# Regrouping VectorE's operations by operand memory while weights are split, with u in PSUM in steps 8 to 21

## The chip, the cores and the metric

The kernel runs on one core of a Trainium2 chip. The core has a matrix engine (PE; its weight loads are shown as PEld), VectorE (DVE), ScalarE (ACT), GpSimd (POOL) and SyncE (SP), which only starts DMAs here. Each engine runs its own list of instructions in order, and semaphores make one wait for another. SBUF is the on-chip memory; PSUM is the smaller memory that PE writes its products into, in eight banks of 512 fp32 columns. POOL works on SBUF alone in this kernel. The metric is the device time of one execution in microseconds (us).

## What is computed

Retention attention on 8 sequences of 576 positions with 8 heads of 64, then a feed-forward layer with a rational activation on the 4608 tokens:

```python
scores = scale * np.matmul(q, k.transpose(0, 1, 3, 2))
Dmat = np.where(rel >= 0, gamma[:, None, None] ** rel[None, :, :], 0.0)
x = np.matmul(scores * Dmat, v)            # then heads side by side: 4608 x 512
h = x @ w_in                               # 512 x 2048
P = a[0] + a[1] * h + a[2] * h**2 + a[3] * h**3
Q = 1.0 + np.abs(b[0]) * np.abs(h) + np.abs(b[1]) * h**2
out = (P / (Q + 1e-6)) @ w_out             # 2048 x 512
```

## The kernel before

All large products are done in a split form: a matrix is kept as a rounded part (hi) and the remainder (lo), and hi·hi, lo·hi and hi·lo are summed. The weights come as 8-byte words and are converted and split on the chip while the first steps already run.

**Steps.** The feed-forward part is a list of steps (b, f): 512 tokens (block b) by 128 columns of w_in (f). Steps 0 to 7 are block 0 with f 0 to 7, steps 8 to 23 block 1 with f 0 to 15, then block 0's other half, then blocks 2 to 8. Step i issues `gemm1` (12 matmuls into a PSUM bank h, two buffers), the activation, and `gemm2` of the step three or four earlier (12 matmuls into acc). The activation of a step:

- `ffn_p`: ACT p = a3·h + a2 and u = |h|; DVE p = p·h ("p·h")
- `ffn_p2`: DVE p = (p + a1)·h ("p2")
- `ffn_v`: ACT v = |b1|·u + |b0|; DVE v = v·u ("v·u")
- `ffn_r`: ACT Ln of v into u, then Exp of u into u (a first reciprocal of Q)
- `ffn_q`: three DVE operations, p = (p + a0)·u, v = (v + 1)·u, p = (v - 2)·p ("q1, q2, q3")
- `ffn_hi`, `ffn_lo`: ACT copies p, rounded, into g's first half; in steps up to 25 POOL, later DVE, subtracts for the second half. g's pool has three buffers.

**Splitting a weight** (`split_weight`) is a generator whose five pieces are `start` (ACT, Abs of the words' high halves into c), `split0` ("shift": one DVE TENSOR_SCALAR on c), `split1` ("low": bits and c), `split2` ("high": bits and c), and `split3` (ACT copies c, rounded, into w, POOL subtracts for w's second half). One or two weights are begun in each step up to 23 (`STARTS`). All operands lie in SBUF.

**Attention** comes in 36 units of 128 positions. `scores` (PE into PSUM ps), `decay` (DVE, ps times a mask into s), in the next step `outputs` (48 small matmuls in the profile), `keep_hi` (ACT, the rounded part into xhi), `keep_lo` (DVE, xlo, and the state S_sb), `fade` (POOL scales S_sb), `scale_q` (POOL) and `scale_v` (ACT, eight instructions on kv). Units 5, 6 and 7 have their scores in steps 1, 3 and 5 and their outputs in steps 2, 4 and 6; unit 4's outputs are in step 0, and unit 8 follows in steps 23 and 24. The pool `ps_at` holds one such ps of two PSUM banks (some early units use `ps_acc`).

**What sets the order.** The lists at the top (lines 33 to 45) are walked in each step by `run`, and each name issues its instructions on the engines it uses; `InOrder` keeps every engine in that order. FIRST holds for steps 0 to 23, DENSE up to step 31, REST after it. Tiles are taken from pools by tag; u and v have two buffers each, p three. The tile framework adds the waits: from what was written to and read from a tile.

Of the kernel before, what the change touches and what calls it, by code (L numbers as in the profile page):

```python
# [12 lines left out]
F32 = mybir.dt.float32  # L13
# [8 lines left out]
P = 128  # L22
# [9 lines left out]

BEFORE = "scale_q split1 scale_v split2 split3 start scores outputs decay split0 keep_hi keep_lo fade".split()
FIRST = (
    "split1 gemm1 outputs ffn_p split2 ffn_hi keep_hi ffn_lo gemm2 ffn_r scale_q split3 keep_lo fade start ffn_p2"
    " scale_v scores decay split0 ffn_q ffn_v"
).split()
DENSE = (
    "gemm1 outputs keep_hi split1 keep_lo fade ffn_p split2 split0 ffn_v scale_q ffn_hi ffn_r ffn_lo scale_v gemm2"
    " ffn_p2 scores decay split3 ffn_q"  # L40
).split()
REST = (
    "gemm1 ffn_p outputs keep_hi keep_lo fade ffn_hi ffn_p2 ffn_lo scores decay scale_q scale_v ffn_v gemm2 ffn_r ffn_q"
).split()
END = "ffn_r ffn_hi gemm2 ffn_lo ffn_q".split()

# [3 lines left out]
SCORES = [1, 3, 5, 23, 25, 27, 29, *range(2 * NF, (NB - 1) * NF, 4)]  # L50
# [16 lines left out]
def retention_ffn(ctx: ExitStack, tc: tile.TileContext, qkv, w_in, w_out, ab, masks, gq, gv, out):  # L67
# [20 lines left out]
    ps_at = ctx.enter_context(tc.tile_pool(name="ps_at", bufs=1, space=PSUM))  # L88
# [184 lines left out]
    els = {}  # L273
    gs = {}
    accs = {}
    part = []
    spare = {}

# [11 lines left out]
    def ffn_p(b, f):  # L290

        h = hs[b, f]
        u, v, p = els[b, f] = [
            (el3 if t == "p" else el).tile([P, 512], F32, tag=t, name=f"{t}{b}_{f}") for t in "uvp"
        ]
        act.activation(p, h, AF.Identity, bias=a2, scale=a3)
        act.activation(u, h, AF.Abs)
        dve.tensor_tensor(p, p, h, ALU.mult)
# [2 lines left out]
        p = els[b, f][2]  # L301
        dve.scalar_tensor_tensor(p, p, a1, hs.pop((b, f)), ALU.add, ALU.mult)

    def ffn_v(b, f):

        u, v, p = els[b, f]
        act.activation(v, u, AF.Identity, bias=b0, scale=b1)
        dve.tensor_tensor(v, v, u, ALU.mult)

    def ffn_r(b, f):  # L310
# [67 lines left out]
    half = NF // 2  # L378
    first = half + NF
    runs = [(0, 0, half), (1, 0, NF), (0, half, NF)] + [(b, 0, NF) for b in range(2, NB)]  # L380
    steps = [(b, f, f == r0, f == r1 - 1) for b, r0, r1 in runs for f in range(r0, r1)]
    at = {s[:2]: i for i, s in enumerate(steps)}

    def lag(i):

        return 4 if NF // 2 <= i < first - 2 or i >= len(steps) - 8 else 3
# [6 lines left out]
    def load_weights(n):  # L393
        for k in [k for _, k in zip(range(n), loads)]:
            load_weight(k)
# [12 lines left out]
    def run(names, todo):  # L408
        todo |= {f"split{j}": (split_step, j) for j in range(4)}
        for name in names:  # L410
            if name in todo:
                todo[name][0](*todo[name][1:])
# [39 lines left out]
    for i in range(len(steps) + lag(len(steps))):  # L452
        this, prev, prev2 = (steps[j][:2] if 0 <= j < len(steps) else None for j in (i, i - 1, i - 2))
        todo = {"gemm2": (products, i), "start": (split_start, STARTS[i] if i < first else 0)}

        out_n = None
        if due and this:
            out_n = due.pop()
            todo |= {f.__name__: (f, out_n) for f in (keep_hi, keep_lo, fade)}
            todo["outputs"] = (put_out, out_n)  # L460
        if i in SCORES:
            todo |= {f.__name__: (f, nxt) for f in (scores, decay)}
            due.append(nxt)
            nxt += 1
        if i + 1 in SCORES:
            todo |= {f.__name__: (f, nxt) for f in (scale_q, scale_v)}
        if this:
            todo |= {f.__name__: (f, *this) for f in (gemm1, ffn_p, ffn_p2, ffn_v)}
        if prev:
            todo |= {f.__name__: (f, *prev) for f in (ffn_r, ffn_q)}  # L470
        if prev2:
            todo |= {"ffn_hi": (ffn_hi, *prev2), "ffn_lo": (ffn_lo, *prev2, i - 2 < first)}
        run(END if not this else FIRST if i < first else DENSE if i < 2 * NF else REST, todo)
        load_weights(2)

# [40 lines left out]
```

## Time and profile before

| | |
|---|---|
| Median of 3 runs | 1001.1 us (1000.58 to 1001.1) |
| The profiled execution | 999.55 us, of which the span from first to last instruction is 997.8 |
| PE busy | 934.3 us (94%) |
| DVE busy | 839.0 us (84%) |
| ACT busy | 709.0 us (71%) |
| POOL busy | 158.3 us (16%) |
| Mean granted TensorE clock | 0.978 |

The engines overlap, so busy times don't add up to the span. What counts is which engine is never free in a stretch of the program, and what the others wait for there. All kernel instructions carry line 63, that of the helper which records them, so they are told apart by the names of their tiles.

### The profile page before, as it was taken

How to read it: one execution, taken by the hardware profiler on the slowest of the kernel's cores; microseconds unless marked ns; L12 is line 12 of the kernel's file. 1: busy time of each engine (PE TensorE's matmuls, PEld its weight loads, DVE VectorE, ACT ScalarE, POOL GpSimd, SP SyncE). 2: the span in 40 equal slices, each digit the busy share in tenths (PEclk: the TensorE clock that was granted, in tenths of full speed). 3: DMA queues.
4: the chain of work that ended last, by engine and by line, in shares of the span. 5: the costliest groups of instructions: out<-in, count | busy, mean ns of one | idle time of the engine just before them, and what ended most of it. 6: DMA issues, size and time to landing. Idle time of an engine off the chain costs nothing.

```text
span 997.8 us, 14766 instructions
## 1 busy us (share of the span) xinstructions
PE 934.3 (94%) x5658; PEld 756.3 (76%) x5658; DVE 839.0 (84%) x1189; ACT 709.0 (71%) x1274; POOL 158.3 (16%) x128
## 2 busy tenths in 40 slices
PE   5687878788999999999999999999999999999998
PEld 5566766566787888878888888888878888888886
DVE  3499989999788888888888888988888888888895
ACT  4386777777767777777777777777777777777774
POOL 2444433443100000100000000100000000000000
PEclk8798999999999999999999999999999999999999
DMA  9943100002212111210121112111211121001001
GB/s 359 407 178 127 43 0 1 1 0 82 89 43 85 44 43 43 85 64 22 43 85 43 43 44 85 43 43 43 85 43 43 43 85 44 1 1 43 1 1 42
DMA packets 20550, 65.31 MB, mean 65 GB/s; under 512 B 2304, under 2 KB 2432, under 8 KB 20480
## 3 DMA queue, kind: packets, MB, share of 16 engines
q1 hardware_dynamic: 20480, 64.37, 17.9%
q8 instruction: 44, 0.72, 0.3%
q14 instruction: 26, 0.21, 0.1%
HBM read 54.93 MB, written 9.44 MB: 65 GB/s over the span
## 4 chain that ended last, share of the span: by engine, by line
PE 73%; DVE 16%; ACT 5%; issue 3%; DMA 2%; POOL 0%; SPq 0%; ACTq 0%; POOLq 0%
PE acc L63 33%; PE h L63 31%; PE ps L63 9%; DVE c L63 7%; DVE p L63 6%; DVE v L63 2%; DMA qk<-in_qkv 2%; ACT c L63 1%; ACT u L63 1%; ACT kv L63 1%; ACT o L63 1%; ACT v L63 1%; DMA kv<-in_qkv 1%; ACT g L63 0%; POOL qk L63 0%
## 5 line engine op out<-in xcount | busy, mean ns | idle before, releaser
L63 PE MATMUL acc<-w,g 128*128 128x512 f32 x1632 | 404.9, 397 | 5.2 <-ACT o L63 4.0
L63 PE MATMUL h<-xhi,w 128*128 128x512 f32 x1152 | 381.1, 392 | 17.9 <-DVE p L63 17.2
L63 PEld LDWEIGHTS acc<-w,g 128*128 128x128 f32 x1632 | 305.2, 190 | 77.4 <-ACT o L63 4.8
L63 PEld LDWEIGHTS h<-xhi,w 128*128 128x128 f32 x1152 | 216.5, 188 | 69.4 <-DVE p L63 22.7
L63 PE MATMUL h<-xlo,w 128*128 128x512 f32 x576 | 224.6, 390 | 0.2 <-DVE xlo L63 0.2
L63 ACT ACTIVATE p<-h,ab_sb 128x512 f32<-128x512 f32 x144 | 111.4, 773 | 135.2 <-PE h L63 135.1
L63 DVE TENSOR_TENSOR v<-v,u 128x512 f32<-128x512 f32 x144 | 124.4, 864 | 27.9 <-ACT v L63 27.9
L63 DVE SCALAR_TENSOR_TENSOR p<-p,ab_sb,u 128x512 f32<-128x512 f32 x144 | 108.8, 756 | 27.2 <-ACT u L63 26.4
L63 ACT ACTIVATE u<-h 128x512 f32<-128x512 f32 x144 | 85.7, 595 | 61.8 <-DVE v L63 60.4
L63 DVE TENSOR_TENSOR p<-p,h 128x512 f32<-128x512 f32 x144 | 98.9, 687 | 33.9 <-ACT u L63 33.2
L63 PEld LDWEIGHTS h<-xlo,w 128*128 128x128 f32 x576 | 108.3, 188 | 22.4 <-DVE xlo L63 0.5
L63 ACT ACTIVATE v<-u,absb 128x512 f32<-128x512 f32 x144 | 116.2, 807 | 1.3 <-DVE p L63 1.1
L63 POOL TENSOR_TENSOR S_sb<-S_sb,gv_sb 128x256 f32<-128x256 f32 x32 | 21.8, 680 | 583.3 <-DVE S_sb L63 583.3
L63 DVE SCALAR_TENSOR_TENSOR p<-p,ab_sb,h 128x512 f32<-128x512 f32 x144 | 107.2, 744 | 3.1
L63 ACT ACTIVATE u<-u,lnb 128x512 f32<-128x512 f32 x144 | 104.4, 725 | 4.7
L63 DVE SCALAR_TENSOR_TENSOR p<-v,p 128x512 f32<-128x512 f32 x144 | 101.6, 706 | 5.0
L63 ACT ACTIVATE u<-v,lnb 128x512 f32<-128x512 f32 x144 | 103.1, 716 | 0.1
L63 DVE SCALAR_TENSOR_TENSOR v<-v,u 128x512 f32<-128x512 f32 x144 | 99.4, 690 | 0.0
L63 ACT ACTIVATE g<-p 128x512 fp32r<-128x512 f32 x136 | 85.7, 630 | 8.0 <-DVE p L63 4.3
L63 DVE TENSOR_TENSOR g<-p,g 128x512 fp32r<-128x512 f32 x112 | 77.6, 693 | 1.4 <-ACT g L63 1.4
L63 ACT ACTIVATE kv<-kv,gv_sb 128x64 f32<-128x64 f32 x288 | 72.5, 340 | 6.2 <-DMA gv_sb<-in_gv 5.0
L63 POOL TENSOR_TENSOR qk<-qk,gq_sb 128x512 f32<-128x512 f32 x36 | 59.7, 1660 | 9.5 <-DMA qk<-in_qkv 9.5
(35 smaller groups left out, 634.6 us busy)
## 6 DMA issues: line engine op xcount, KB each, us to landing
qk<-in_qkv SPq DMA_DIRECT2D x36, 512.0 KB, 4.8
kv<-in_qkv SPq DMA_DIRECT2D x36, 512.0 KB, 3.9
bits<-in_w_in SPq DMA_DIRECT2D x16, 512.0 KB, 10.2
bits<-in_w_out SPq DMA_DIRECT2D x16, 512.0 KB, 10.2
out<-o SPq DMA_DIRECT2D x16, 512.0 KB, 3.2
out<-o SPq DMA_DIRECT2D x4, 256.0 KB, 2.3
gq_sb<-in_gq SPq DMA_DIRECT2D x1, 256.0 KB, 2.7
mask_sb<-in_masks SPq DMA_DIRECT2D x1, 128.0 KB, 4.5
```

The source lines that it names most:

```text
L63: return lambda *a, **k: self.tc.keep_in_program_order(method(*a, **k))
```

## The change

Three things are changed. The order FIRST is a new one, in which `scores` and `decay` stand last, `outputs` stays near the front, and the three DVE pieces of a split follow each other behind `ffn_q`. In steps up to 23 `ffn_r` works on the step's own u and v, not on those of the step before, and `ffn_hi` on the step before, not on the one before that; step 24 then has neither. And in steps 8 to 21 u is one of the two halves (banks) of a tile free_at, which is taken from `ps_at` in step 8 and given up in step 22. `ffn_v` is cut in two, `ffn_va` (ACT) and `ffn_v` (DVE); in DENSE and REST the two stand together.

```diff
 FIRST = (
-    "split1 gemm1 outputs ffn_p split2 ffn_hi keep_hi ffn_lo gemm2 ffn_r scale_q split3 keep_lo fade start ffn_p2"
-    " scale_v scores decay split0 ffn_q ffn_v"
+    "gemm1 outputs ffn_p ffn_lo keep_hi split3 ffn_va ffn_p2 ffn_v keep_lo fade ffn_r start ffn_q ffn_hi"
+    " split0 split1 split2 scale_q scale_v gemm2 scores decay"
 ).split()
...
+    free_at = []
...
         u, v, p = els[b, f] = [
+            free_at[f % 2] if t == "u" and free_at else
             (el3 if t == "p" else el).tile([P, 512], F32, tag=t, name=f"{t}{b}_{f}") for t in "uvp"
         ]
...
-    def ffn_v(b, f):
+    def ffn_va(b, f):
 
         u, v, p = els[b, f]
         act.activation(v, u, AF.Identity, bias=b0, scale=b1)
+
+    def ffn_v(b, f):
+        u, v, p = els[b, f]
         dve.tensor_tensor(v, v, u, ALU.mult)
...
-            todo |= {f.__name__: (f, *prev) for f in (ffn_r, ffn_q)}
+            todo["ffn_q"] = ffn_q, *prev
+
+        if i != first and (this if i < first else prev):
+            todo["ffn_r"] = ffn_r, *(this if i < first else prev)
+        if i != first and (prev if i < first else prev2):
+            todo["ffn_hi"] = ffn_hi, *(prev if i < first else prev2)
         if prev2:
-            todo |= {"ffn_hi": (ffn_hi, *prev2), "ffn_lo": (ffn_lo, *prev2, i - 2 < first)}
+            todo["ffn_lo"] = ffn_lo, *prev2, i - 2 < first
+        if i == half:
+            ps = ps_at.tile([P, 2, 512], F32, tag="at", name="free_at")
+            free_at.extend((ps[:, 0], ps[:, 1]))
+        elif i == SCORES[3] - 1:
+            free_at.clear()
```

Three places in the built order show it. The first is DVE in step 12 (block 1, f = 4) before: the rows of one step, each with the semaphores that it waits for in brackets (Activation is ACT's).

```order
L63 SCALAR_TENSOR_TENSOR c_11_1199<-bits_11_862,c_11_1199 128x512 [waits DMAHW7_49]
L63 TENSOR_TENSOR p_4_1228<-p_4_1228,h_4_1213 128x512 [waits Activation_49,Pool_49]
L63 SCALAR_TENSOR_TENSOR c_11_1199<-bits_11_862,c_11_1199 128x512 [waits DVE_49]
L63 SCALAR_TENSOR_TENSOR p_4_1228<-p_4_1228,ab_sb,h_4_1213 128x512 [waits DVE_49]
L63 TENSOR_SCALAR c_8_1255<-c_8_1255 128x512 [waits Activation_49]
L63 SCALAR_TENSOR_TENSOR p_3_1170<-p_3_1170,ab_sb,u_3_1168 128x512
L63 SCALAR_TENSOR_TENSOR v_3_1169<-v_3_1169,u_3_1168 128x512
L63 SCALAR_TENSOR_TENSOR p_3_1170<-v_3_1169,p_3_1170 128x512 [waits DVE_49]
L63 TENSOR_TENSOR v_4_1227<-v_4_1227,u_4_1226 128x512 [waits Activation_49]
```

The same step in the changed kernel:

```order
L63 TENSOR_TENSOR p_4_1229<-p_4_1229,h_4_1215 128x512 [waits Activation_49,Pool_49]
L63 SCALAR_TENSOR_TENSOR p_4_1229<-p_4_1229,ab_sb,h_4_1215 128x512 [waits DVE_49]
L63 TENSOR_TENSOR v_4_1228<-v_4_1228,free_at 128x512 [waits Activation_49]
L63 SCALAR_TENSOR_TENSOR p_3_1172<-p_3_1172,ab_sb,free_at 128x512 [waits Activation_49]
L63 SCALAR_TENSOR_TENSOR v_3_1171<-v_3_1171,free_at 128x512
L63 SCALAR_TENSOR_TENSOR p_3_1172<-v_3_1171,p_3_1172 128x512 [waits DVE_49]
L63 TENSOR_SCALAR c_8_1242<-c_8_1242 128x512 [waits Activation_49]
L63 SCALAR_TENSOR_TENSOR c_8_1242<-bits_8_952,c_8_1242 128x512 [waits DMAHW0_49,DVE_49]
L63 SCALAR_TENSOR_TENSOR c_8_1242<-bits_8_952,c_8_1242 128x512 [waits DVE_49]
```

The c rows have moved from between p's rows to the end of the step, and the row that forms p_3 from u (q1), which had no wait, now waits for ACT.

The second place is ACT in the same step of the changed kernel (g_3 and p_3 are the step before's; w_11 is a weight that was begun in the step before).

```order
L63 ACTIVATE p_4_1229<-h_4_1215,ab_sb 128x512 [waits PE_49,Pool_49]
L63 ACTIVATE free_at<-h_4_1215 128x512 [waits Activation_49]
L63 ACTIVATE w_11_1234<-c_11_1185 128x512 [waits DVE_49,Activation_49]
L63 ACTIVATE v_4_1228<-free_at,absb 128x512 [waits Activation_49]
L63 ACTIVATE free_at<-v_4_1228,lnb 128x512 [waits DVE_49]
L63 ACTIVATE free_at<-free_at,lnb 128x512 [waits Activation_49]
L63 ACTIVATE c_8_1242<-bits_8_952 128x512 [waits DMAHW0_49]
L63 ACTIVATE g_3_1247<-p_3_1172 128x512 [waits DVE_49,PE_49]
```

Ln and Exp (the two rows with lnb) now follow v of the same step, where they were those of the step before; g is that of the step before, and it also waits for PE, whose product frees its buffer.

The third place is DVE where step 3 ends and step 4 begins, in the changed kernel; s_696 is `decay` of unit 6, c the weight begun in step 3, and xlo comes from `keep_lo` of unit 6.

```order
L63 TENSOR_SCALAR c_3_663<-c_3_663 128x512 [waits Activation_49]
L63 SCALAR_TENSOR_TENSOR c_3_663<-bits_3_537,c_3_663 128x512 [waits DMAHW4_49,DVE_49]
L63 SCALAR_TENSOR_TENSOR c_3_663<-bits_3_537,c_3_663 128x512 [waits DVE_49]
L63 TENSOR_TENSOR s_696<-ps_687,mask_sb 128x1024 [waits PE_49]
L63 TENSOR_TENSOR p_4_745<-p_4_745,h_4_702 128x512 [waits Activation_49,Pool_49]
L63 SCALAR_TENSOR_TENSOR p_4_745<-p_4_745,ab_sb,h_4_702 128x512 [waits DVE_49]
L63 TENSOR_TENSOR v_4_744<-v_4_744,u_4_743 128x512 [waits Activation_49]
L63 TENSOR_TENSOR xlo_446<-ps_687,xhi_445 128x4x128 [waits PE_49]
```

Before, the row of s stood behind p2 of step 3, with the shift, q1 to q3, v·u and the low operation between it and step 4's p·h; now p·h follows it at once.

More of the change, by code (lines that the diff above doesn't have):

```diff
@@ L34 @@
 FIRST = (
-    "split1 gemm1 outputs ffn_p split2 ffn_hi keep_hi ffn_lo gemm2 ffn_r scale_q split3 keep_lo fade start ffn_p2"
-    " scale_v scores decay split0 ffn_q ffn_v"
+    "gemm1 outputs ffn_p ffn_lo keep_hi split3 ffn_va ffn_p2 ffn_v keep_lo fade ffn_r start ffn_q ffn_hi"
+    " split0 split1 split2 scale_q scale_v gemm2 scores decay"
 ).split()
 DENSE = (
-    "gemm1 outputs keep_hi split1 keep_lo fade ffn_p split2 split0 ffn_v scale_q ffn_hi ffn_r ffn_lo scale_v gemm2"
+    "gemm1 outputs keep_hi split1 keep_lo fade ffn_p split2 split0 ffn_va ffn_v scale_q ffn_hi ffn_r ffn_lo scale_v gemm2"
     " ffn_p2 scores decay split3 ffn_q"
@@ L42 @@
 REST = (
-    "gemm1 ffn_p outputs keep_hi keep_lo fade ffn_hi ffn_p2 ffn_lo scores decay scale_q scale_v ffn_v gemm2 ffn_r ffn_q"
+    "gemm1 ffn_p outputs keep_hi keep_lo fade ffn_hi ffn_p2 ffn_lo scores decay scale_q scale_v ffn_va ffn_v gemm2 ffn_r ffn_q"
 ).split()
@@ L302, in ffn_p2 @@
         dve.scalar_tensor_tensor(p, p, a1, hs.pop((b, f)), ALU.add, ALU.mult)
+    def ffn_va(b, f):
+        u, v, p = els[b, f]
+        act.activation(v, u, AF.Identity, bias=b0, scale=b1)
     def ffn_v(b, f):
         u, v, p = els[b, f]
-        act.activation(v, u, AF.Identity, bias=b0, scale=b1)
         dve.tensor_tensor(v, v, u, ALU.mult)
@@ L467, in retention_ffn @@
         if this:
-            todo |= {f.__name__: (f, *this) for f in (gemm1, ffn_p, ffn_p2, ffn_v)}
+            todo |= {f.__name__: (f, *this) for f in (gemm1, ffn_p, ffn_p2, ffn_va, ffn_v)}
         if prev:
-            todo |= {f.__name__: (f, *prev) for f in (ffn_r, ffn_q)}
-        if prev2:
-            todo |= {"ffn_hi": (ffn_hi, *prev2), "ffn_lo": (ffn_lo, *prev2, i - 2 < first)}
+            todo["ffn_q"] = ffn_q, *prev
[3 more added lines that the diff above has]
+            todo["ffn_hi"] = ffn_hi, *(prev if i < first else prev2)
+        if prev2:
+            todo["ffn_lo"] = ffn_lo, *prev2, i - 2 < first
[4 more added lines that the diff above has]
+            free_at.clear()
         run(END if not this else FIRST if i < first else DENSE if i < 2 * NF else REST, todo)
```

## The prediction

> **What bounds the kernel now.** I read the page's forty slices and its chain first, then busy time by stretch, then the timeline of one step on each engine. In the slices each digit is the tenths of 24.9 us for which an engine is busy.
>
> ```profile
> PE   5687878788999999999999999999999999999998
> DVE  3499989999788888888888888988888888888895
> PE 73%; DVE 16%; ACT 5%; issue 3%; DMA 2%; POOL 0%; SPq 0%; ACTq 0%; POOLq 0%
> ```
>
> From the tenth slice on PE is full, and the order of the work there stays as it was. Ahead of that VectorE (DVE) is full and PE is not; the chain gives DVE 16%, 160 us. The next view cuts the first part where p·h (`ffn_p`) starts in steps 0 and 8 and in step 22; behind each stretch stand its length and the busy time of PE, PEld, DVE, ACT and POOL.
>
> ```profile
> 49.00:116.40 67.40, 55.53 (x396) 44.57 (x392) 65.66 (x91) 51.63 (x97) 31.57 (x25) 0.92 0.36 134
> 116.40:218.20 101.80, 83.18 (x343) 63.93 (x341) 92.13 (x127) 74.39 (x115) 39.81 (x29) 0.98 0.00 1
> 248.60:997.80 749.20, 739.51 (x4433) 601.40 (x4431) 634.69 (x908) 541.00 (x962) 57.24 (x50) 1.00 0.14 48
> ```
>
> So steps 0 to 7 take 67.4 us, steps 8 to 21 take 101.8 us (14 steps, 7.27 each), and DVE is what is never free. The rest, 749 us, is PE's. Now one ordinary step of the second stretch as DVE runs it, then ACT and POOL around it (start, duration).
>
> ```profile
> 145.43 0.69 DVE L63 SCALAR_TENSOR_TENSOR c<-bits,c 128x512 int32<-128x512 int32 x1
> 146.03 0.68 DVE L63 TENSOR_TENSOR p<-p,h 128x512 f32<-128x512 f32 x1
> 146.63 1.19 DVE L63 SCALAR_TENSOR_TENSOR c<-bits,c 128x512 int32<-128x512 int32 x1
> 147.74 0.73 DVE L63 SCALAR_TENSOR_TENSOR p<-p,ab_sb,h 128x512 f32<-128x512 f32 x1
> 149.07 1.07 DVE L63 TENSOR_SCALAR c<-c 128x512 int32<-128x512 int32 x1 [0.60 <-ACT c L63]
> 150.06 0.74 DVE L63 SCALAR_TENSOR_TENSOR p<-p,ab_sb,u 128x512 f32<-128x512 f32 x1
> 150.72 0.68 DVE L63 SCALAR_TENSOR_TENSOR v<-v,u 128x512 f32<-128x512 f32 x1
> 151.44 0.69 DVE L63 SCALAR_TENSOR_TENSOR p<-v,p 128x512 f32<-128x512 f32 x1
> 152.05 0.68 DVE L63 TENSOR_TENSOR v<-v,u 128x512 f32<-128x512 f32 x1
> 152.65 0.68 DVE L63 SCALAR_TENSOR_TENSOR c<-bits,c 128x512 int32<-128x512 int32 x1
> ...
> 144.94 0.63 ACT L63 ACTIVATE g<-p 128x512 fp32r<-128x512 f32 x1
> 145.55 0.72 ACT L63 ACTIVATE u<-v,lnb 128x512 f32<-128x512 f32 x1
> 146.31 0.72 ACT L63 ACTIVATE u<-u,lnb 128x512 f32<-128x512 f32 x1
> 147.85 0.63 ACT L63 ACTIVATE w<-c 128x512 fp32r<-128x512 f32 x1 [0.82 <-DVE c L63]
> 148.39 0.65 ACT L63 ACTIVATE c<-bits 128x512 f32<-128x512 f32 x1
> 148.95 0.80 ACT L63 ACTIVATE v<-u,absb 128x512 f32<-128x512 f32 x1
> 151.50 0.60 ACT L63 ACTIVATE u<-h 128x512 f32<-128x512 f32 x1 [1.08 <-DVE v L63]
> 152.16 0.64 ACT L63 ACTIVATE g<-p 128x512 fp32r<-128x512 f32 x1
> ...
> 145.71 1.56 POOL L63 TENSOR_TENSOR g<-p,g 128x512 fp32r<-128x512 f32 x1 [3.07 <-issue]
> 148.56 1.30 POOL L63 TENSOR_TENSOR w<-c,w 128x512 fp32r<-128x512 f32 x1 [1.29 <-PE acc L63]
> ```
>
> The period is 152.65 - 145.43 = 7.22 us. In the change's words the c rows are shift (TENSOR_SCALAR), low (first with bits) and high (second). High takes 1.19 instead of low's 0.69: POOL's g had begun and ends at 147.27, and high ends 0.55 later. POOL itself waited: low ended at 146.12, and from there g takes 1.15. The shift takes 1.07 and ends at 150.14, 0.28 behind POOL's w (149.86). With 0.60 of idle ahead of it, 0.50 + 0.60 + 0.61 = 1.7 us of a step are port and wait, where the undisturbed shift is half of this pair, 0.46:
>
> ```profile
> 59.02 0.92 DVE L63 TENSOR_SCALAR c<-c 128x512 int32<-128x512 int32 x2
> 62.46 2.39 DVE L63 SCALAR_TENSOR_TENSOR c<-bits,c 128x512 int32<-128x512 int32 x2
> 62.68 1.62 POOL L63 TENSOR_TENSOR g<-p,g 128x512 fp32r<-128x512 f32 x1 [3.35 <-ACT g L63]
> 76.27 1.28 DVE L63 SCALAR_TENSOR_TENSOR c<-bits,c 128x512 int32<-128x512 int32 x2
> ```
>
> The lower three rows decide much. Two lows back to back take 1.28 alone, but 2.39 when POOL's g comes during the first. 2.39 is 0.68 + 1.16 + 0.55: **a POOL subtraction that is waiting goes in between two DVE operations that need the port.** p·h, with one operand in PSUM, ran beside POOL (146.03, 0.68).
>
> **Steps 9 to 21 in the new order.** DVE now runs p·h, p2, v·u, then q1, q2, q3 (`ffn_q` of the step before), shift, low, high. Read with its waits, the order shows that q1 waits for ACT although v·u, just before it, already waited for ACT's v. Only Ln and Exp of the *same* step come next on ACT and touch free_at, in its other half. q1's own u was ready a step ago. So q1 waits for an Exp that it doesn't need, and the step closes in one ring, each piece by the rows above (0.02 per hand-over, 0.04 between dependent DVE operations, as 151.40 to 151.44):
> - high ends, w 0.02 + 0.54 (147.85 to 148.39), v 0.80, v·u 0.02 + 0.68: 2.06
> - Ln 0.02 + 0.76 (145.55 to 146.31), Exp 0.72: 3.56
> - q1 0.02 + 0.66, q2 0.72, q3 0.61 to the next start: 5.57
> - shift 0.46 + 0.04, low 0.68 + 0.04, high 0.68: 7.47.
>
> POOL's w falls beside p2 and v·u, which now read PSUM: free. But POOL's g does not. q3 ends, ACT copies g (0.03, as 152.13 to 152.16, and 0.63), POOL begins 0.13 later (145.57 to 145.71): 0.79 behind q3. Low runs from 0.42 to 1.10 behind q3. So g takes the port at 1.10, holds it 1.15, and high ends at 2.80 in place of 1.82: +0.98, **8.45 us a step**. Against 7.22, 13 steps: +16.0. ACT's reads from PSUM are 0.03 shorter (u 0.60 against w 0.63), for v and Exp: -0.07 x 13 = -0.9. Writing to PSUM from ACT has no row; the shortest row of this width (0.60) against Ln's 0.72 bounds it at 0.12 either way for Ln and Exp, 13 x 0.24 = 3 us; I take nothing, as reads change by only 0.03. **Term: +15**, from +1 (7.47, PSUM writes fast) to +18.
>
> A page speaks for the move. The Trainium skill, "ScalarE: Activation LUTs", section "Step-by-step: what each stage is for", calls ScalarE's way to PSUM the lower-latency one; it gives no figure, and no run here shows it. By it the term would go towards the lower of the bounds above.
>
> **Steps 0 to 7.** Here u stays in SBUF and q1 has no such wait. What changes is the attention unit: `scores` and `decay` now stand last in a step, and `outputs`, which needs decay, first in the next (0, 2, 4, 6). Before, this is what lay between:
>
> ```profile
> 57.89 1.22 DVE L63 TENSOR_TENSOR s<-ps,mask_sb 128x1024 f32<-128x1024 f32 x1
> ...
> 59.21 1.24 PE L63 MATMUL ps<-s,kv 128*64 128x128 f32 x16 [2.69 <-ACT c L63]
> 60.17 1.13 PE L63 MATMUL ps<-kv 128*64 128x64 f32 x16
> 61.23 1.13 PE L63 MATMUL ps<-qk,S_sb 64*64 64x128 f32 x16
> ...
> 62.51 0.58 ACT L63 ACTIVATE xhi<-ps 128x512 fp32r<-128x512 f32 x1
> 62.99 0.71 ACT L63 ACTIVATE u<-v,lnb 128x512 f32<-128x512 f32 x1
> ```
>
> From decay's end (59.11) to xhi are 3.40 us, hidden behind the shifts, q1 to q3 and v·u. Now behind decay DVE has only p·h and p2 (0.60 + 0.04 + 0.74 = 1.38). v·u needs ACT's v, and ACT stands at xhi: 3.40 + 0.48 + w 0.54 + v 0.82 = 5.24. DVE idles 3.86 in each of four steps: +15.4. The port: g between low and high costs 0.98 here too, v·u (u in SBUF) meets POOL's w, and q2 and q3 meet fade and scale_q, which now follow keep_lo directly; gone are the stalls of high and of the shifts (0.50 and 0.61 in the step above). I count 0.8 more a step, +6. If none of DVE's regrouped work met POOL, 8 x 1.1 would go instead. **Term: +21**, from +7 to +25.
>
> **Steps 22 to 24.** Step 24 runs in the old DENSE order, but its `outputs` waits for a decay that now ends step 23, and p and u of step 24 stand behind xhi on ACT: two of the three PE groups (2.1), xhi 0.48, p and u 1.3, 3.9 us with 0.6 of DVE work (keep_lo). Before, DVE had q, v·u and a split there. +3.3; step 22's v·u meets POOL again, +1. **Term: +4**, 2 to 6. Later steps keep their order; `ffn_va` stands where `ffn_v` began. PE's order is the same throughout. g's buffer now waits for the product four steps back, done by then: 0.
>
> **The sum.** 15 + 21 + 4 = +40 on this execution's 999.55 (span 997.8); the median, 1001.1, lies 1.55 higher: **1041 us**.
>
> **The rivals.** (a) DVE keeps the port from low to high. For it: high follows within 0.04. Against it: the 2.39 row. It saves 0.98 in 13 + 7 steps, 20 us: 1021.
> (b) q1 doesn't wait for the other half's Exp. The Trainium skill, "PSUM — Partial Sum Buffer", section "PSUM bank collisions raise a hardware error", asks engines to be kept apart by bank, and the halves are two banks: by that rule the wait is not needed. Worked from the rows, the ring then runs Exp, ACT's c (0.63 behind Exp's start: 0.72 less the overlap of 0.09 from 148.39 to 148.95; 0.66 long), shift, low, high with g, 7.04 a step, -2 in place of +15: 1024. Against it: the wait stands in the built order.
> (c) The other side, faster: the port is all that DVE loses. If the 1.7 us of 14 steps and some 1.1 of 8 go (24 + 9) and q1's wait lies under other work, while the idle behind decay stays (15.4 + 4): 1001 - 33 + 19 = 987. It decides where q1's wait and the port in steps 9 to 21 cost together under 1.7; I count 1.6 (q1 could start at 1.98 in the ring, and starts at 3.58) and 0.98.
> That the grouping doesn't keep POOL away from the SBUF operations is part of my forecast.
>
> **How the numbers follow.** Forecast (1028 to 1052) 0.73, (a) 0.13, (b) 0.04, (c) 0.05, no change 0.03, beyond 1052 0.02. The range goes from under (a) to the upper bounds of all terms, 1018 to 1052. A measurement of this kernel tells 0.2% from no change: faster 0.05, same 0.03, slower 0.92.
>
> **What would show it.** Right: starts of p·h 8.4 apart in steps 9 to 21, an idle of 1.5 on DVE ahead of q1 released by ACT's free_at, high at 1.6 to 1.7; in steps 2, 4 and 6 an idle of some 4 ahead of v·u. Wrong: high at 0.68 (a), no idle ahead of q1 (b), a step under 7.2 (c).

## The result, and the profile after

The changed kernel takes 1047.33 us (median of 4 runs, 1044.29 to 1047.96) against 1001.1 for the kernel before (1000.58 to 1003.93): ratio 1.0446, 95% interval 1.0431 to 1.0462. It is slower by 46 us, the predicted side; the predicted time was 1041.

First the page of the changed kernel, the same three lines as before: busy tenths of PE and DVE in 40 slices (26.2 us each now), and the shares of the chain that ended last.

```profile
PE   6645694977699999999999999999999999999998
DVE  2377897888778888888888988898888888888895
PE 71%; DVE 12%; ACT 10%; issue 5%; POOL 1%; DMA 0%; SPq 0%; ACTq 0%; POOLq 0%; DVEq 0%
```

PE is full from the twelfth slice on (288 us). Before, it was full from the eleventh (249 us; the prediction says the tenth, but that digit is an 8). Ahead of that, DVE now has mostly 7 and 8 where 9 stood. ACT's share of the chain goes from 5% to 10%, DVE's from 16% to 12%. So the time is lost in the first 300 us, where DVE waits for ACT more than before. The view of busy time by stretch says how much and where (cut at the first p·h, at those of steps 8, 22 and 26, and at the end; behind each stretch its length, the busy time of PE, PEld, DVE, ACT and POOL, then the granted clock of PE as a share of full speed, the DMA share and GB/s):

```profile
53.42:144.29 90.87, 57.95 (x397) 47.09 (x393) 74.01 (x94) 51.89 (x98) 35.84 (x26) 0.83 0.22 82
144.29:261.69 117.40, 86.94 (x344) 67.18 (x343) 94.61 (x128) 72.10 (x114) 36.90 (x28) 0.91 0.00 1
261.69:298.63 36.94, 26.88 (x175) 21.32 (x174) 28.30 (x37) 21.69 (x45) 11.52 (x9) 0.86 0.15 50
298.63:1046.20 747.57, 738.02 (x4433) 600.31 (x4431) 634.97 (x908) 541.28 (x962) 56.93 (x50) 1.00 0.14 48
```

The kernel before has its starts of p·h in the same steps at 49.00, 116.36, 218.21 and 248.52; the stretch of it that was not shown yet is that of steps 22 to 25:

```profile
218.21:248.52 30.31, 26.01 (x177) 20.21 (x176) 27.96 (x38) 22.38 (x47) 12.68 (x10) 0.94 0.18 57
```

| | before | after | difference | predicted |
|---|---|---|---|---|
| to the first p·h | 49.00 | 53.42 | +4.4 | 0 |
| steps 0 to 7 | 67.36 | 90.87 | +23.5 | +21 |
| steps 8 to 21 | 101.85 | 117.40 | +15.6 | +15 |
| steps 22 to 25 | 30.31 | 36.94 | +6.6 | +4 |
| the rest | 749.28 | 747.57 | -1.7 | 0 |
| span | 997.80 | 1046.20 | +48.4 | +40 |

Steps 0 to 25 together are 46 us longer. In them DVE is busy for 11 us more, and idle for 35 us more. In steps 0 to 7 alone it is busy for 8.4 more (74.0 against 65.7) and idle for 15.1 more.

Now an ordinary step of the second stretch in the changed kernel, DVE, ACT and POOL in order of start (start, duration; in brackets the idle time ahead and what ended it, "issue" where the profile shows nothing that did; "x2" is two operations back to back, here low and high).

```profile
165.49 0.63 ACT L63 ACTIVATE g<-p 128x512 fp32r<-128x512 f32 x1 [1.62 <-DVE p L63]
165.77 2.36 DVE L63 SCALAR_TENSOR_TENSOR c<-bits,c 128x512 int32<-128x512 int32 x2
...
166.26 1.32 POOL L63 TENSOR_TENSOR g<-p,g 128x512 fp32r<-128x512 f32 x1 [4.43 <-ACT g L63]
...
168.22 0.63 ACT L63 ACTIVATE w<-c 128x512 fp32r<-128x512 f32 x1 [0.95 <-DVE c L63]
168.76 0.76 ACT L63 ACTIVATE v<-free_at,absb 128x512 f32<-128x512 f32 x1
168.76 0.75 DVE L63 SCALAR_TENSOR_TENSOR p<-p,ab_sb,h 128x512 f32<-128x512 f32 x1
168.93 1.27 POOL L63 TENSOR_TENSOR w<-c,w 128x512 fp32r<-128x512 f32 x1 [1.35 <-ACT w L63]
169.55 0.69 DVE L63 TENSOR_TENSOR v<-v,free_at 128x512 f32<-128x512 f32 x1
170.28 0.69 ACT L63 ACTIVATE free_at<-v,lnb 128x512 f32<-128x512 f32 x1 [0.76 <-DVE v L63]
171.00 0.66 ACT L63 ACTIVATE free_at<-free_at,lnb 128x512 f32<-128x512 f32 x1
...
171.69 0.75 DVE L63 SCALAR_TENSOR_TENSOR p<-p,ab_sb,free_at 128x512 f32<-128x512 f32 x1 [1.45 <-ACT free_at L63]
```

Here the reader sees the ring go round: high, w, v, v·u, Ln, Exp, then q1 after an idle of 1.45. POOL's w lies beside p2 and v·u, which run at 0.75 and 0.69, undisturbed. POOL's g comes while low runs, goes in between, and low and high take 2.36.

And step 2, with the attention unit's products (PE), its copy xhi, and what stands behind it on ACT:

```profile
74.13 1.98 PE L63 MATMUL ps<-s,kv 128*64 128x128 f32 x16 [11.01 <-issue]
...
78.09 0.60 ACT L63 ACTIVATE xhi<-ps 128x512 fp32r<-128x512 f32 x1 [7.52 <-PE ps L63]
78.59 1.14 ACT L63 ACTIVATE w<-c 128x512 fp32r<-128x512 f32 x2
...
79.63 0.81 ACT L63 ACTIVATE v<-u,absb 128x512 f32<-128x512 f32 x1
80.47 0.69 DVE L63 TENSOR_TENSOR v<-v,u 128x512 f32<-128x512 f32 x1 [5.06 <-ACT v L63]
```

DVE stands still for 5.06 us, because v sits in ACT's queue behind xhi, and xhi waits for the products that decay releases.

### The profile page after: what moved, and what is told of

Same layout as the page of the kernel before. It is cut to its first block, busy times and chain, and to the rows that moved or that the text cites. A ratio compares the mean times of both kernels' runs of the same rounds, so it can differ in the third digit from the quotient of the medians.

```text
span 1046.2 us, 14809 instructions
## 1 busy us (share of the span) xinstructions
PE 945.1 (90%) x5658; PEld 766.7 (73%) x5658; DVE 848.7 (81%) x1189; ACT 706.4 (68%) x1274; POOL 156.1 (15%) x128
## 4 chain that ended last, share of the span: by engine, by line
PE 71%; DVE 12%; ACT 10%; issue 5%; POOL 1%; DMA 0%; SPq 0%; ACTq 0%; POOLq 0%; DVEq 0%
PE acc L63 31%; PE h L63 29%; PE ps L63 11%; DVE c L63 4%; DVE v L63 4%; DVE p L63 3%; ACT free_at L63 2%; ACT v L63 2%; ACT u L63 2%; ACT w L63 2%; ACT kv L63 1%; POOL qk L63 1%; ACT o L63 1%; ACT p L63 1%; ACT xhi L63 0%
## 5 line engine op out<-in xcount | busy, mean ns | idle before, releaser
L63 PEld LDWEIGHTS acc<-w,g 128*128 128x128 f32 x1632 | 304.3, 189 | 88.0 <-ACT o L63 13.9
L63 DVE TENSOR_TENSOR v<-v,u 128x512 f32<-128x512 f32 x130 | 120.1, 924 | 41.6 <-ACT v L63 40.9
L63 DVE SCALAR_TENSOR_TENSOR p<-p,ab_sb,u 128x512 f32<-128x512 f32 x130 | 99.3, 763 | 27.4 <-ACT u L63 26.4
L63 ACT ACTIVATE v<-u,absb 128x512 f32<-128x512 f32 x130 | 105.0, 807 | 0.4
L63 ACT ACTIVATE u<-h 128x512 f32<-128x512 f32 x130 | 77.2, 594 | 39.6 <-DVE v L63 38.1
L63 ACT ACTIVATE u<-v,lnb 128x512 f32<-128x512 f32 x130 | 93.1, 716 | 13.1 <-DVE v L63 13.0
L63 ACT ACTIVATE u<-u,lnb 128x512 f32<-128x512 f32 x130 | 94.3, 726 | 4.2
L63 DVE SCALAR_TENSOR_TENSOR v<-v,u 128x512 f32<-128x512 f32 x130 | 91.2, 701 | 0.0
L63 PE MATMUL ps<-s,kv 128*64 128x128 f32 x576 | 46.4, 311 | 40.6 <-issue 38.8
```

Source lines behind the costliest of these rows:

```text
L63: return lambda *a, **k: self.tc.keep_in_program_order(method(*a, **k))
```

## The experiments

Three costs were claimed: q1's wait, the port between low and high, and the idle behind decay. Each is taken out alone, then together; after that the place of u is tried in three orders. All totals are medians, and the ratio is against the kernel before, timed on the same chip; the times of stretches and steps are those of the profiled execution.

### 1. Two tiles in place of two halves

Each bank of u becomes a tile of its own. `ps_at` is closed for steps 8 to 22 and opened again in step 23, so the number of banks is the same.

```diff
-    ps_at = ctx.enter_context(tc.tile_pool(name="ps_at", bufs=1, space=PSUM))
+    at_stack = ctx.enter_context(ExitStack())
+    ps_at = at_stack.enter_context(tc.tile_pool(name="ps_at", bufs=1, space=PSUM))
...
         if i == half:
-            ps = ps_at.tile([P, 2, 512], F32, tag="at", name="free_at")
-            free_at.extend((ps[:, 0], ps[:, 1]))
+            at_stack.close()
+            ps_u = at_stack.enter_context(tc.tile_pool(name="ps_u", bufs=1, space=PSUM))
+        if half <= i < SCORES[3] - 1:
+            free_at[:] = [ps_u.tile([P, 512], F32, tag=f"u{i % 2}", name=f"free_at{i % 2}")] * 2
...
+        elif i == SCORES[3]:
+            at_stack.close()
+            ps_at = at_stack.enter_context(tc.tile_pool(name="ps_at2", bufs=1, space=PSUM))
```

> The changed kernel, but u's two PSUM banks are two tiles instead of the halves of one; same order, same banks, same operations. Theory (the step is closed by a wait for the other half's Exp, which tracking of one tile adds): the idle of 1.45 us ahead of q1 goes, VectorE becomes the bound with p.h 0.60, p2 0.74, v.u 0.68, q1 0.66, q2 0.72, q3 0.61, shift 0.50, low and high 2.36 together, about 7.0 us a step in place of 8.4: steps 9 to 21 lose 13 x 1.4 = 18 us, so some 1029 us. Low and high still take 2.36 together. Rival (b) of the prediction, turned round: the idle has another source (ACT's g or Ln is late by itself) and appears ahead of v.u or shift instead: 8.4 us a step and 1047 us. Rival (the idle is only half of it, since ACT then becomes the bound): between 7.5 and 8 us a step, 1035 to 1042 us.

Measured: 1029.13 us, ratio 1.0268 (1.0249 to 1.0287). Steps 8 to 21 take 100.11 us in place of 117.40; the other stretches stay (90.90 and 37.07). DVE and ACT in a step (the last row is low and high of this step):

```profile
155.38 0.69 DVE L63 TENSOR_TENSOR v<-v,free_at 128x512 f32<-128x512 f32 x1
155.99 0.74 DVE L63 SCALAR_TENSOR_TENSOR p<-p,ab_sb,free_at 128x512 f32<-128x512 f32 x1
...
156.83 0.66 ACT L63 ACTIVATE free_at<-free_at,lnb 128x512 f32<-128x512 f32 x1
...
158.58 2.36 DVE L63 SCALAR_TENSOR_TENSOR c<-bits,c 128x512 int32<-128x512 int32 x2
```

q1 now starts 0.61 behind v·u, ahead of Exp and not after it: the idle is gone, and most steps take about 7.0 us. The wait had been one between two banks, made by treating both as one tile. The 2.36 of low and high is as before.

### 2. The new order with u in SBUF

The lines that take free_at are left out, nothing else.

```diff
-        if i == half:
-            ps = ps_at.tile([P, 2, 512], F32, tag="at", name="free_at")
-            free_at.extend((ps[:, 0], ps[:, 1]))
-        elif i == SCORES[3] - 1:
-            free_at.clear()
```

> The changed kernel with its new order, but u stays in SBUF in steps 8 to 21 as in the others. Theory (ring through Exp, closed by the shared PSUM tile): u then has two tiles, the idle ahead of q1 goes; v.u meets POOL's w in SBUF now, some 0.5 us a step, so 7.5 to 7.6 us a step in place of 8.4 and about 1037 us; the second part of the change, as built, costs more than it saves. Rival (u in PSUM is what keeps POOL away from v.u, q1 and q2 and so pays for itself): 8.4 us a step or more, 1047 us or above. Rival (the order alone sets the step): 8.4 us again, 1047 us.

Measured: 1039.21 us, ratio 1.0372 (1.0353 to 1.0391); 7.6 us in an ordinary step. Both rivals fall: with u in SBUF the changed kernel is 8 us faster, so its second part, as built, costs more than it saves.

### 3. g behind v

`ffn_hi` and `ffn_lo` are issued together behind ACT's v, one step later.

```diff
-    "gemm1 outputs ffn_p ffn_lo keep_hi split3 ffn_va ffn_p2 ffn_v keep_lo fade ffn_r start ffn_q ffn_hi"
+    "gemm1 outputs ffn_p keep_hi split3 ffn_va ffn_hi ffn_lo ffn_p2 ffn_v keep_lo fade ffn_r start ffn_q"
...
-        if i != first and (prev if i < first else prev2):
-            todo["ffn_hi"] = ffn_hi, *(prev if i < first else prev2)
         if prev2:
+            todo["ffn_hi"] = ffn_hi, *prev2
```

> The changed kernel, but g (ACT's copy and POOL's subtraction) is issued behind v's ACT operation, one step later, so that POOL's g stands beside p2 and v.u and not beside low. Theory (a waiting POOL subtraction goes in between two VectorE operations that need the port): low and high back to back take 1.3 us in place of 2.36, the ring through Exp stays, so 7.4 to 7.5 us a step in steps 9 to 21 in place of 8.4 (13 us), and some 0.5 a step in steps 0 to 7 (4 us): about 1030 us. Rival (a) of the prediction (VectorE keeps the port from low to high, and the 1.65 us of high has another cause, such as its own words' DMA): low and high stay at 2.36, 1047 us. Rival (the 1 us of the port lies under the wait for Exp): low and high 1.3 but still 8.4 us a step, 1047 us.

Measured: 1028.37 us, ratio 1.0265 (1.0247 to 1.0282). Steps 0 to 7 take 87.99, steps 8 to 21 103.58. In a step:

```profile
167.38 1.42 DVE L63 SCALAR_TENSOR_TENSOR c<-bits,c 128x512 int32<-128x512 int32 x2
...
170.22 0.69 DVE L63 TENSOR_TENSOR v<-v,free_at 128x512 f32<-128x512 f32 x1
170.85 1.28 POOL L63 TENSOR_TENSOR g<-p,g 128x512 fp32r<-128x512 f32 x1
...
172.37 0.75 DVE L63 SCALAR_TENSOR_TENSOR p<-p,ab_sb,free_at 128x512 f32<-128x512 f32 x1 [1.45 <-ACT free_at L63]
```

Low and high fall from 2.36 to 1.42, the step from 8.40 to 7.43, and q1's idle stays at 1.45. POOL's g now lies in that idle. The two costs stand in one ring, one behind the other, and each is paid in full.

### 4. scores and decay behind v·u

```diff
-    "gemm1 outputs ffn_p ffn_lo keep_hi split3 ffn_va ffn_p2 ffn_v keep_lo fade ffn_r start ffn_q ffn_hi"
-    " split0 split1 split2 scale_q scale_v gemm2 scores decay"
+    "gemm1 outputs ffn_p ffn_lo keep_hi split3 ffn_va ffn_p2 ffn_v scores decay keep_lo fade ffn_r start ffn_q ffn_hi"
+    " split0 split1 split2 scale_q scale_v gemm2"
```

> The changed kernel, but scores and decay stand behind v.u of their step rather than last. Theory (the attention's chain behind decay, 3.4 us and 0.5 for xhi, is no longer covered by VectorE work): the idle of about 4 us ahead of v.u in steps 0, 2, 4 and 6 goes, steps 0 to 7 take some 80 us in place of 91 and steps 22 to 25 some 31 in place of 37, steps 9 to 21 stay at 8.4 each: about 1030 us. Rival (the first steps wait for weights or DMA, and decay's place only decides where the idle is seen): steps 0 to 7 stay near 91 us and the whole at 1045 to 1047 us. Also told here: from the start to the first p.h the changed kernel took 4.4 us more than the one before, with the same order there; if that is a matter of the execution, the start varies between the profiles of kernels that are equal up to there.

Measured: 1023.96 us, ratio 1.0221 (1.0206 to 1.0236). Steps 0 to 7 take 77.02, 22 to 25 take 30.16 (before: 30.31), steps 8 to 21 117.13. So the idle behind decay cost 13.9 us in steps 0 to 7, and in steps 22 to 25 it was the whole loss. What is left of the loss in steps 0 to 7, 9.7 us, is for the most part DVE beside POOL: DVE is busy for 73.9 us there, 8.2 more than before. Here the stretch, and then rows of step 2:

```profile
50.34:127.36 77.02, 57.05 (x400) 45.08 (x394) 73.90 (x93) 52.20 (x98) 34.90 (x26) 0.93 0.31 114
...
70.17 2.50 POOL L63 TENSOR_TENSOR w<-c,w 128x512 fp32r<-128x512 f32 x2 [1.95 <-ACT w L63]
...
71.43 1.78 DVE L63 TENSOR_TENSOR v<-v,u 128x512 f32<-128x512 f32 x1
...
75.24 1.70 POOL L63 TENSOR_TENSOR qk<-qk,gq_sb 128x512 f32<-128x512 f32 x1
75.86 1.64 DVE L63 SCALAR_TENSOR_TENSOR p<-v,p 128x512 f32<-128x512 f32 x1
```

With u in SBUF, v·u takes 1.78 beside POOL's w and q3 1.64 beside scale_q (the row of qk); undisturbed they take 0.69. q2, between the two, takes 1.10 beside fade, and undisturbed 0.68.

### 5. Experiments 1 and 3 together

> Two edits together on the changed kernel: u's banks as two tiles, and g issued behind v. Measured alone they took 18 us and 19 us off the changed kernel. Theory (two separate costs, the wait for Exp and the port between low and high): both go, p.h 0.60, p2 0.74, v.u 0.68, q1 0.66, q2 0.72, q3 0.61, shift 0.50, low and high 1.3, about 6.0 us a step in steps 9 to 21, 1012 us. Rival (either edit already gives all that there is, since another engine is next at 7 us): 7.0 us a step, about 1024 us.

Measured: 1015.51 us, ratio 1.014 (1.0118 to 1.0162); 6.04 us in an ordinary step, 87.87 in steps 8 to 21. The costs add up in a step (8.40 - 1.39 - 0.97 = 6.04). The whole is 3.5 us above what I expected; 2.4 of it lie in steps 11 and 12, which take 7.28 and 7.24 us and had been counted as ordinary ones.

### 6. All three together

> The three edits together: two tiles for u, g behind v, scores and decay behind v.u. Theory (three separate costs, and the change's grouping is sound below them): steps 0 to 7 some 75 us (before: 67), steps 8 to 21 some 86 us (before: 102), steps 22 to 25 some 31 (before: 30): about 990 us, faster than the kernel before by 1%. Rival (what is taken off in steps 8 to 21 comes back as a wait of PE, of weights' DMA or in step 22 and later): steps 8 to 21 as short, but the rest longer than 750 us, and 1000 us or above.

Measured: 991.95 us, ratio 0.9904 (0.9885 to 0.9922), faster than the kernel before. The busy time by stretch, from the first p·h:

```profile
52.27:123.71 71.44, 57.18 (x399) 45.38 (x394) 68.03 (x94) 51.57 (x97) 34.08 (x25) 0.93 0.30 111
123.71:211.44 87.73, 77.17 (x325) 62.11 (x326) 82.17 (x127) 70.82 (x114) 35.70 (x28) 0.96 0.00 1
...
242.43:990.20 747.77, 738.03 (x4433) 600.42 (x4431) 634.60 (x908) 541.57 (x962) 57.44 (x50) 1.00 0.14 48
```

and one step (p·h starts at 175.16, and again at 181.20, 6.04 later):

```profile
175.16 0.68 DVE L63 TENSOR_TENSOR p<-p,h 128x512 f32<-128x512 f32 x1
...
176.04 1.30 POOL L63 TENSOR_TENSOR w<-c,w 128x512 fp32r<-128x512 f32 x1 [3.49 <-ACT w L63]
...
176.67 0.69 DVE L63 TENSOR_TENSOR v<-v,free_at 128x512 f32<-128x512 f32 x1
177.27 0.74 DVE L63 SCALAR_TENSOR_TENSOR p<-p,ab_sb,free_at 128x512 f32<-128x512 f32 x1
177.29 1.31 POOL L63 TENSOR_TENSOR g<-p,g 128x512 fp32r<-128x512 f32 x1
```

POOL's w and g both lie beside operations that read PSUM. Steps 8 to 21 take 14 us less than before, with DVE busy for 82.2 us in place of 92.2: that is what the grouping is worth here, with u in PSUM and g moved. Nothing of it is given back later (747.8 against 749.3). Steps 0 to 7 remain 4.1 us above the kernel before; what of POOL's work would have to move there was not tried.

### 7. keep_hi behind p2 as well

The edit is shown against experiment 6.

```diff
-    "gemm1 outputs ffn_p keep_hi split3 ffn_va ffn_hi ffn_lo ffn_p2 ffn_v scores decay keep_lo fade ffn_r start ffn_q"
+    "gemm1 outputs ffn_p split3 ffn_va ffn_hi ffn_lo ffn_p2 keep_hi ffn_v scores decay keep_lo fade ffn_r start ffn_q"
```

> As the three edits together, and keep_hi (ACT's copy to xhi, which waits for the attention's products) behind p2 in the list, so that ACT's w and v are not queued behind it. Theory (ACT in order at xhi is what holds up v.u in steps 0, 2, 4 and 6): steps 0 to 7 shorter by 1 to 3 us than with the three edits alone, the rest unchanged, about 988 us. Rival (v.u is held up by VectorE's own queue): no difference, within 1 us.

Measured: 992.14 us, ratio 0.9902 (0.9883 to 0.9921): no difference to experiment 6. Steps 0 to 7 take 70.58 in place of 71.44, less than the 1 to 3 us that the theory wanted, and within the 1 us of its rival. With decay early there was next to nothing left to gain: in experiment 6 DVE's idle ahead of v·u is 0.46 in step 0 and 0.47 in step 4, and under 0.1 in steps 2 and 6.

### 8. The old order with u in PSUM

The free_at lines of the change are put into the kernel before, whose order stays.

```diff
+    free_at = []
...
+            free_at[f % 2] if t == "u" and free_at else
...
+        if i == half:
+            ps = ps_at.tile([P, 2, 512], F32, tag="at", name="free_at")
+            free_at.extend((ps[:, 0], ps[:, 1]))
+        elif i == SCORES[3] - 1:
+            free_at.clear()
```

> The kernel before, with its old order, and only u put into the halves of free_at in steps 8 to 21. Theory (the tile's false wait costs something only where Exp of the same step is queued ahead of q1, as in the new order; in the old order Exp(i-1) and q1(i-1) belong together anyway, and VectorE's stalls there are high beside POOL's g and the shift beside POOL's w, neither of which has u): 7.2 us a step as before, within 0.1, and 999 to 1003 us. Rival (u in PSUM gains by itself, ACT's and VectorE's operations on it shorter): 7.0 us a step or less, 998 us or below. Rival (the shared tile costs here too, by a wait of ACT's u for v.u of the step before): 7.5 us or more, 1005 us or above.

Measured: 1013.32 us, ratio 1.0117 (1.0096 to 1.0138), 8.2 us a step: my theory missed. I had looked for the wait only where Exp stands ahead of q1. The trace shows it elsewhere (q2 of one step, then ACT's v of the next):

```profile
147.62 0.68 DVE L63 SCALAR_TENSOR_TENSOR v<-v,free_at 128x512 f32<-128x512 f32 x1
...
148.33 0.78 ACT L63 ACTIVATE v<-free_at,absb 128x512 f32<-128x512 f32 x1 [2.36 <-DVE v L63]
```

Both only read free_at, and in different halves; still v starts when q2 ends, 2.36 us after ACT was free. So not only a write and a read are kept apart, but two reads by two engines too. The Trainium skill, "PSUM — Partial Sum Buffer", section "PSUM bank collisions raise a hardware error", asks for this within one bank, reads included. Here the wait reaches over two banks, which the Trainium skill does not ask for; in experiments 1 and 10, with a tile for each bank, it is gone.

### 9. The three edits with u in SBUF

Experiment 6 without its lines for `ps_u` and free_at.

> The new order with g behind v and decay behind v.u (as in the three edits together), but u in SBUF in steps 8 to 21. Theory (putting u in PSUM is worth something once it costs no wait: v.u, q1 and q2 then read PSUM and don't meet POOL's w and g): with u in SBUF v.u and q1 meet POOL's w and g, 6.6 to 7.2 us a step in place of 6.05, so 1000 to 1008 us. Rival (POOL's subtractions lie beside p.h and p2 alone, u's place is without effect once the order is mended): 6.05 us a step and 992 us.

Measured: 1006.49 us, ratio 1.0056 (1.0034 to 1.0077); 7.46 us a step, 104.34 in steps 8 to 21. POOL and DVE in a step:

```profile
182.38 1.28 POOL L63 TENSOR_TENSOR w<-c,w 128x512 fp32r<-128x512 f32 x1 [4.46 <-ACT w L63]
...
183.04 1.17 DVE L63 TENSOR_TENSOR v<-v,u 128x512 f32<-128x512 f32 x1
183.66 1.70 POOL L63 TENSOR_TENSOR g<-p,g 128x512 fp32r<-128x512 f32 x1
184.13 1.77 DVE L63 SCALAR_TENSOR_TENSOR p<-p,ab_sb,u 128x512 f32<-128x512 f32 x1
```

v·u takes 1.17 and q1 1.77, where experiment 6's rows have 0.69 and 0.74 with u in PSUM, beside the same work of POOL. That is 1.5 us, about as much as the step is longer (7.46 against 6.04). Once it costs no wait, u in PSUM is worth 14.5 us.

### 10. The old order with two tiles

Experiment 8 with the tiles of experiment 1.

> The old order with u in PSUM in steps 8 to 21 as two one-bank tiles in place of the halves of one. With the halves of one, the old order took 8.21 us a step and 1013 us, against my expectation of 7.2: there ACT's v of a step (reading one half) waited for q2 of the step before (reading the other half), two reads, and came 2.36 us late. Theory (the wait is one for the tile as a whole and falls away with two tiles): 7.2 us a step as before, 999 to 1003 us. Rival (the old order pays for u in PSUM in another way, by slower operations or the bank): 8.2 us a step, 1013 us. Rival (PSUM as place of u gains in the old order too): below 7.0 us a step, below 998 us.

Measured: 998.66 us, ratio 0.9986 (0.9975 to 0.9998); 7.20 us a step. The 2.36 ahead of v is gone:

```profile
150.42 0.76 ACT L63 ACTIVATE v<-free_at,absb 128x512 f32<-128x512 f32 x1
150.55 1.06 DVE L63 TENSOR_SCALAR c<-c 128x512 int32<-128x512 int32 x1 [0.60 <-ACT c L63]
```

In the old order u's place gains next to nothing, since it is the shift and high that meet POOL there, and neither has u.

Orders against the place of u in steps 8 to 21, in us:

| | u in SBUF | halves of one tile | two tiles |
|---|---|---|---|
| old order | 1001.1 | 1013.3 | 998.7 |
| new order | 1039.2 | 1047.3 | 1029.1 |
| new order, g behind v | - | 1028.4 | 1015.5 |
| new order, g behind v, decay behind v·u | 1006.5 | - | 992.0 |

## Why the prediction was right, and where it was off

**Steps 8 to 21, predicted +15, measured +15.6.** The ring was right piece by piece: it gave 8.45 us a step, and ordinary steps take 8.40. Experiment 1 shows q1's wait (1.39 a step), experiment 3 the port (0.97, counted as 0.98).

**ACT and PSUM.** The Trainium skill, "ScalarE: Activation LUTs", section "Step-by-step: what each stage is for", calls ScalarE's way to PSUM the lower-latency one. The trace agrees by a little: Ln, which reads SBUF, takes 0.69 to PSUM against 0.72 to SBUF. Exp takes 0.66 against 0.72, but it reads from PSUM as well. At 13 steps and 0.09 the two give 1.2 us, near the zero that I took and far from the 3 of the bound.

**Steps 0 to 7, predicted +21, measured +23.5.** Both terms have the right cause, and both were off in size, in opposite directions. The idle behind decay was counted as "3.86 in each of four steps", 15.4. There are only three such steps. In step 0 DVE idles for 0.46 ahead of v·u, less than the 0.91 of the kernel before, and in steps 2 (shown above), 4 and 6 for 5.06, 4.17 and 4.53:

```profile
55.35 0.69 DVE L63 TENSOR_TENSOR v<-v,u 128x512 f32<-128x512 f32 x1 [0.46 <-ACT v L63]
...
104.58 1.18 DVE L63 TENSOR_TENSOR v<-v,u 128x512 f32<-128x512 f32 x1 [4.17 <-ACT v L63]
...
129.47 1.18 DVE L63 TENSOR_TENSOR v<-v,u 128x512 f32<-128x512 f32 x1 [4.53 <-ACT v L63]
```

The three make 13.8, and experiment 4 gets back 13.9. That this lies so near 15.4 is in part luck: one idle too many was counted, and each of the three was taken too short. In step 2 the reasons can be read: two weights are split there (w takes 1.14, not 0.54), and the first sixteen products take 1.98, not 1.24, at a lower granted clock. Over the sixteen products alone (74.1 to 76.1) it is 0.50; the busy time by stretch of the changed kernel has 0.56 as the mean of the 6 us around them:

```profile
73.00:79.00 6.00, 4.87 (x52) 4.32 (x53) 2.37 (x3) 0.91 (x2) 0.00 (x0) 0.56 0.00 0
```

The port was counted as "0.8 more a step", +6, and 9.7 us remain with decay early, 8.2 of them as longer operations of DVE. Moving g takes 5.6 of the 9.7 (77.02 in experiment 4 against 71.44 in experiment 6). Where POOL still comes in then, the rows of experiment 4 show: at v·u, q2 and q3, with all operands in SBUF. This is the term that was set too low.

**Steps 22 to 25, predicted +4, measured +6.6.** Right cause: with decay early the stretch takes 30.16. The size was off in part for the same reason as above. Step 24's `outputs` in the changed kernel:

```profile
279.58 1.97 PE L63 MATMUL ps<-s,kv 128*64 128x128 f32 x16 [8.12 <-issue]
...
282.69 0.60 ACT L63 ACTIVATE xhi<-ps 128x512 fp32r<-128x512 f32 x1 [6.41 <-PE ps L63]
```

From the first product to xhi are 3.11 us, where I counted 2.1 for the two groups; the granted clock is 0.50 over the first group (279.5 to 281.5). That is 1.0 of the 2.6 that the term was short; the rest was not traced.

**The start, +4.4, not predicted.** The first p·h is at 53.42 in the changed kernel's profile and at 48.97 in experiment 1's, whose order is the same up to there; the profiles of the ten experiments lie between 48.97 and 52.27. So this is put down to the execution and not to the change, as far as single profiles can tell. Without it the profile gives +44; the medians give +46.

**The rivals.** (a) falls: low and high take 2.36 while POOL's g comes with low and 1.42 once it comes elsewhere, so a waiting POOL subtraction does go in between. (b) was wrong for the changed kernel and right as a sum: it gave 7.04 us a step without the wait, and experiment 1 measured 7.0; there the shift starts 0.04 behind ACT's c, as (b) has it. (c), the faster side, had the right idea of what the grouping is worth but not of its terms: it needs all three edits, and then comes to 992, not 987.

**Slips in the working.** The lower bound of the first term, +1, does not follow from its rows: 13 x 0.25 less 0.9 and less 3 is -0.7. The upper bounds 18, 25 and 6 add up to 1050, not 1052. No working is given for the 25. The forecast of 1041 does not rest on any of these.

## What to carry to other kernels

Where two buffers share one PSUM tile, an access of one engine may wait for the other engine's access to the other half, reads too; a tile for each bank took away 18 us here, and 15 us in the old order. Grouping VectorE's SBUF operations gained little here (7.0 us a step in experiment 1, 7.2 in experiment 10) until GpSimd's g was moved away from the group (6.04). So ask of each GpSimd operation when its input comes, since one that arrives during the group goes in between. When an order is rewritten, follow each chain that leaves the engine (here decay, products, xhi) and count what lies over it before and after.

## What was not expected of the hardware

- VectorE's operations with one operand in PSUM ran undisturbed beside GpSimd (v·u 0.69, q1 0.74 in experiment 6); with all in SBUF they took 1.17 and 1.77. The Trainium skill, "SBUF — State Buffer", section "Summary: rules for kernel authors", says that a VectorE operation with two SBUF inputs and a GpSimd one that reads SBUF block each other, the second until the first is done. The trace agrees for a single pair: v·u of experiment 9 ends at 184.21, 0.55 behind POOL's w (183.66). But a group on VectorE does not keep GpSimd out: GpSimd got its turn between two operations that stood back to back, at 0.94 us a time (2.36 against 1.42).
- PE's first sixteen products of step 2 took 1.24 us in the kernel before, behind an idle of PE of 2.69, at a granted clock of 0.84 (59.2 to 60.4 us). In the changed kernel they took 1.98, behind an idle of 11.01, at 0.50 (74.1 to 76.1). The two groups that follow run at 0.50 in both kernels and take about the same (1.13 and 1.13 before, 1.10 and 1.13 after). That the longer idle is what lowered the clock was not tried; if so, a delay on VectorE lengthened the very chain that VectorE waited for.
